# The inverse of chunks 0 to 3 in blocks of 16 instead of one back substitution over 32

## The chip, the cores and the metric

The kernel runs on one core of one Trainium2 chip. The metric is the device time of one launch in microseconds (us), taken as the median of several runs. A profile is one such execution, recorded instruction by instruction; it has a span of its own.

## What is computed

The reference is a recurrent attention block (RWKV-7) with an activation block behind it. Shapes: batch 4, 8 heads, 768 steps, head dimension 40; then 3072 tokens of width 320 through a layer of width 2048.

```python
for t in range(S):                     # per batch and head, state is D x D
    y[t] = r[t] @ state
    Sa = state @ a[t]                  # einsum('bhde,bhe->bhd')
    state = state * w[t][None, :] - outer(Sa, b[t]) + outer(v[t], k[t])
x = y as (3072, 320)
h = x @ w_in
out = (h * cos(h)) @ w_out
```

`w_in` and `w_out` arrive as float64; everything else is float32.

## The kernel before

**Chunks.** The 768 steps are cut into 24 chunks of C = 32 steps. The four batches lie in four blocks of 32 partitions, so one instruction works on 4 batches, and 8 heads lie along the free axis. Within a chunk the recurrence becomes a triangular system: for each batch and head a 32x32 strictly triangular matrix N of products of a and b (decays put in) is needed, and the inverse of the unit triangular matrix made of it. Inverses are made for four chunks at a time, which is 4 x 4 x 8 = 128 systems, one to a partition.

**The steps of a chunk** (names as in the code). `p1_w`, `p1_a`, `p1_b`, `p1_n` prepare two chunks at once: transposed decays `wb`, `aT`, `bT`, and in `p1_n` the products `nps`, which ACT copies into `nt` (L447). `p2_v`, `p2_k`, `p2_g` transpose v, r, k and make the `gram` products, masked by DVE into `ag` and `vvm`. `ch_t` transposes the states `qz`; `ch_q` multiplies them by r; `ch_x` makes the right-hand sides `x0`; `ch_s` multiplies them by the inverse `rt` (products `sps`) and has ACT and DVE take them to `sm`; `ch_z` makes the new states (`dps`; DVE adds at L656 and L663, POOL multiplies by the decay at L657 and L668).

**The inverse.** `inv_start` transposes `nt` into `u` (L460), so that each partition holds one system. `inv_step(j)` for j = 31 down to 1 is one step of back substitution: an outer product of j by (32 - j) elements into `inv_tmp` (L468), and its subtraction from `inv` (L472). `inv_end` transposes `inv` back into `rt` (L476), four chunks in one tile. All of it runs on DVE.

**The weights.** 20 pieces of 128 x 512 float64 numbers are rounded to float32 in the kernel, in four kinds of step: fetch (SP issues the DMA into a tile `words`, L233), taken (DVE L241 and L242, ACT L245 and L247), mantissa (DVE L251, ACT L254), product (DVE L257, POOL L260 for the sign). The `words` tiles share buffers with other tiles: pieces 0 and 1 with `gT`, 2 with `nt`, 3 with `u`, 4 with `inv`, so that pieces 2, 3 and 4 can be fetched only when the first inverse is through with these. The parts of `w_in_sb` and `w_out_sb` that are written last serve as early buffers for w, a and b of chunks 2 and 3.

**The order.** The program is scheduled by hand: each engine runs its instructions in the order in which the Python code issues them, and waits on semaphores where data are missing. `step(work, of_inv, of_w)` does one segment, then counts down the waiting jobs given to `later(n, job)` (mostly loads, to be issued n segments on), then takes `of_inv` steps off the list `inv_steps` and `of_w` off the list `w_steps`. The loop over c at the end lists the segments of each chunk; `M` stands for a place where a piece of the activation block (`first_a`, `first_b`, `second`: products `ph` and `po`) is done. The prologue before it does the preparation of chunks 0 to 3, the inverse, and v, k, g of chunks 0 and 1. SP's queue issues nearly all loads, in order. `busy(n)` issues n matmuls on zeros, and `shifted(n)` n tiny ones on PE.

Lines that matter below: L170 and L175 the scan of decays, L180 its store to `wd` and L152 the loads of w, a, b, k, v, r, L392 `bn`, L490 the POOL copies `vp` and `rp`, L497 and L498 `kn` and v in `vvm`, L541 and L547 the masks of gram, L600 DVE's copy of `x0`, L732 and L740 DVE's part of the cosine.

Of the kernel before, what the change touches and what calls it, by code (L numbers as in the profile page):

```python
# [9 lines left out]
F32 = mybir.dt.float32  # L10
# [10 lines left out]
def kernel(  # L21
# [43 lines left out]
    nc = tc.nc  # L65
# [50 lines left out]

    late = DFF - 2 * H * DP
    late_out = w_out_sb.rearrange("p f n -> p (f n)")[:, NF * DM - 2 * H * DP :]
    nat = {}
    for n, fill in (("w", 1.0), ("a", 0.0), ("b", 0.0)):  # L120
        for i in range(4):
# [310 lines left out]
    def p1_n(c):  # L432
        ps = at("nps")
        for i in range(2):
            for j in range(4):
                for bb in range(B):
                    for e in range(2):
                        mm(
                            ps[blk[bb ^ e], e, (4 * i + j) * C : (4 * i + j + 1) * C],
                            G["bT", c + i][half[e], j, blk[bb]], G["aT", c + i][half[e], j, blk[bb]],  # L440
                            i == 0 and j == 0,
                        )

        if c % 4 == 0:
            G["nt"] = sb1.tile([P, C, 4, 2, HH], F32, tag="nt", name="nt")
        for e in range(2):
            nc.scalar.copy(  # L447
                G["nt"][:, :, c % 4 : c % 4 + 2, e, :].rearrange("p t c j -> p c j t"),
                ps[:, e, : 2 * HH * C].rearrange("p (c j t) -> p c j t", c=2, j=HH),
            )  # L450
        if c % 4 == 2:
            G["inv"] = sb1.tile([P, C * C], F32, tag="inv", name="inv")
            nc.gpsimd.memset(G["inv"], 0.0)
            nc.gpsimd.memset(G["inv"][:, :: C + 1], -1.0)
# [16 lines left out]
        )  # L471
        nc.vector.tensor_tensor(x[:, j:, :j], x[:, j:, :j], tmp, ALU.subtract)  # L472

    def inv_end(c):
        rt = sb2.tile([P, 4, H, C], F32, tag="rt", name="rt")
        nc.vector.transpose(  # L476
            rt.rearrange("p c h t -> p t (c h)"), G["inv"].rearrange("p (t s) -> p t s", t=C)
        )
        for i in range(4):
            G["rt", c + i] = rt[:, i]  # L480

    def inverse(c):
        return [
# [324 lines left out]
    def scanned(q):  # L808

        ws_scan(q)  # L810
        later(2, lambda: ws_store(q))
        if q + 1 < NCH // 4:
            later(12, lambda: ws_fetch(q + 1))
# [17 lines left out]
    with tc.manual_schedule():  # L831
# [46 lines left out]
        first, other = p1(0), p1(2)  # L878
        for seg in (*first[:2], *other[:2], *first[2:], *other[2:]):
            step(seg)  # L880
        scanned(1)
        p2_in(0)
        p2_kn(0)
        inv_steps.extend(inverse(0))
        v, k, g = p2(0)
        v1, k1, g1 = p2(1)
        for n, seg in ((12, v), (0, k), (0, g), (6, main(0)[2]), (6, None), (4, v1), (0, k1), (0, g1)):
            for _ in range(n):
                inv_steps.pop(0)()
            if seg:  # L890
                step(seg)
            else:
                for m in range(3):
                    w_work[m][0]()
                p2_in(1)
                p2_kn(1)
        N_PAD = {0: 111, 19: 75}
        shifted(N_PAD[0])
        while inv_steps:
            inv_steps.pop(0)()  # L900
            if 2 < len(inv_steps) < 9:
                busy(1, True)
        for m in range(3, 5):
            w_work[m][0]()

        done = 0

# [9 lines left out]
            return done < len(pieces) and 2 * pieces[done][0] + 2 <= c  # L917

        M = object()
        for c in range(NCH):  # L920
            t, q, x, s, z = main(c)
            v, k, g = p2(c + 1) if c + 1 < NCH else [lambda: None] * 3
            q0 = c - c % 4 + 4
            fill, pn, pn4 = (1, 4), None, None
            if c == 0:
                segs = [s, z]
            elif c == 1:
                segs = [t, v, q, k, x, g, s, z]
            elif c == 2:
                segs, fill = [t, v, q, k, M, x, M, g, M, s, M, z, M, M], (0, 2)  # L930
            elif c == 3:
                pw4, pa4, pb4, pn4 = p1(4)
                pw, pa, pb, pn = p1(6)
# [39 lines left out]
            for i, seg in enumerate(segs):  # L973
                while seg is s and ("rt", c) not in G:
                    if allowed(c):
                        piece(4, 0)
                    else:
                        inv_steps.pop(0)()
                while seg is pn4 and w_steps:
                    w_steps.pop(0)()  # L980
                if seg is not M:
                    step(seg, *fill, small=seg in (q, x, g, s, z, pn, pn4))
                    if c < 2 or c == 2 and not done:
                        busy({s: 6, q: 5, v: 4, k: 4, z: 4}.get(seg, 3))
                else:
                    place += 1
                    if place * empty // places > (place - 1) * empty // places:
                        continue
                    if allowed(c) and (c != 4 or done < 23):
                        piece(*fill)  # L990
                while i == n - 1 and c > 3 and done < goal and c != 4 and allowed(c):
                    piece(*fill)
                if seg is pn and (c == 3 or c > 4 and c % 4 == 2):
                    inv_steps.extend(inverse(q0))
# [36 lines left out]
```

## Time and profile before

Three runs took 819.85, 822.35 and 826.33 us; the median is 822.35.

| | |
|---|---|
| median of the runs | 822.35 us |
| span of the profiled execution | 823.7 us (mean granted TensorE clock 0.948) |
| PE busy | 746.9 us, 91% of the span |
| PE weight loads | 571.3 us, 69% |
| DVE busy | 509.3 us, 62% |
| ACT busy | 383.8 us, 47% |
| POOL busy | 201.3 us, 24% |
| the inverse's steps on DVE | L472: 72.0 us x186, L468: 70.0 us x186 |
| HBM | 42.07 MB read, 11.14 MB written |

The page also cuts the span into 40 slices of 20.6 us and gives the busy share of each in tenths:

```profile
PE   3656778899689999999999999999999999999997
DVE  6987887859645599354797553895444874332231
PEclk9757799899789999999999999999999999999999
```

The first eight to ten slices are the start: the first chunks, the first inverse and the rounding of the weights. Then PE's row stays at 9.

A row of a table of groups has line, engine, operation, tiles written and read, shapes, count, then busy time. A row of a timeline has start, length, engine, line, operation, tiles, and in brackets the idle time of the engine before it and what ended it. A row of the chain of waits has start, length and who held the chain; SPq and PEq are queues, "issue" is time in which an engine waited for nothing that the profile shows.

### The profile page before, as it was taken

How to read it: one execution, taken by the hardware profiler on the slowest of the kernel's cores; microseconds unless marked ns; L12 is line 12 of the kernel's file. 1: busy time of each engine (PE TensorE's matmuls, PEld its weight loads, DVE VectorE, ACT ScalarE, POOL GpSimd, SP SyncE). 2: the span in 40 equal slices, each digit the busy share in tenths (PEclk: the TensorE clock that was granted, in tenths of full speed). 3: DMA queues.
4: the chain of work that ended last, by engine and by line, in shares of the span. 5: the costliest groups of instructions: out<-in, count | busy, mean ns of one | idle time of the engine just before them, and what ended most of it. 6: DMA issues, size and time to landing. Idle time of an engine off the chain costs nothing.

```text
span 823.7 us, 37673 instructions
## 1 busy us (share of the span) xinstructions
PE 746.9 (91%) x16832; PEld 571.3 (69%) x16832; DVE 509.3 (62%) x1081; ACT 383.8 (47%) x707; POOL 201.3 (24%) x352
## 2 busy tenths in 40 slices
PE   3656778899689999999999999999999999999997
PEld 2534456677467777778777777777787777777775
DVE  6987887859645599354797553895444874332231
ACT  1214676544244553545446446435635445363352
POOL 5315554430214023212221230330330222201000
PEclk9757799899789999999999999999999999999999
DMA  8456663244043322333223323214310212101000
GB/s 120 78 132 168 173 162 104 46 119 69 25 98 84 64 59 52 69 100 65 54 37 71 68 63 67 61 37 65 66 41 24 45 35 52 21 21 37 20 17 16
DMA packets 183297, 55.66 MB, mean 68 GB/s; under 512 B 157152, under 2 KB 178656, under 8 KB 183136
## 3 DMA queue, kind: packets, MB, share of 16 engines
q1 hardware_dynamic: 180560, 51.95, 29.2%
q8 instruction: 132, 2.16, 1.1%
q10 hardware_dynamic: 2320, 0.98, 0.6%
q0 software_dynamic: 256, 0.33, 0.2%
q14 instruction: 29, 0.24, 0.1%
HBM read 42.07 MB, written 11.14 MB: 65 GB/s over the span
## 4 chain that ended last, share of the span: by engine, by line
PE 63%; DVE 19%; ACT 6%; DMA 4%; issue 3%; SPq 3%; POOL 1%; DVEq 0%; ACTq 0%; POOLq 0%
PE ph L101 22%; PE po L101 20%; DVE inv_tmp L468 4%; DVE inv L472 4%; PE x0ps L101 3%; PE dps L101 3%; SPq L152 3%; PE gram L101 2%; DVE rw L391 2%; PE vT L326 2%; PE sps L101 2%; PE qps L101 1%; DVE turns L732 1%; PE nps L101 1%; PE sT L558 1%
## 5 line engine op out<-in xcount | busy, mean ns | idle before, releaser
L101 PE MATMUL po<-w_out_sb,gT 128*128 128x320 f32 x768 | 227.0, 445 | 0.0
L101 PE MATMUL ph<-xT,w_in_sb 128*128 128x256 f32 x768 | 189.5, 393 | 4.8 <-DVE gT L740 3.8
L101 PEld LDWEIGHTS po<-w_out_sb,gT 128*128 128x128 f32 x768 | 142.4, 193 | 55.9 <-issue 4.2
L101 PEld LDWEIGHTS ph<-xT,w_in_sb 128*128 128x128 f32 x768 | 142.3, 194 | 33.9 <-issue 13.9
L730 ACT ACTIVATE turns<-ph,rnd 128x512 f32<-128x512 f32 x96 | 63.8, 685 | 157.2 <-PE ph L101 156.7
L732 DVE SCALAR_TENSOR_TENSOR turns<-turns,ph 128x512 f32<-128x512 f32 x96 | 63.8, 684 | 109.2 <-ACT turns L730 108.9
L740 DVE TENSOR_TENSOR gT<-ph,turns 128x512 f32<-128x512 f32 x96 | 65.6, 685 | 36.3 <-ACT turns L737 36.3
L657 POOL TENSOR_TENSOR qz<-qz,wc 128x160 f32<-128x160 f32 x92 | 43.2, 489 | 163.1 <-DVE qz L656 162.6
L472 DVE TENSOR_TENSOR inv<-inv,inv_tmp 128x31 f32<-128x31 f32 (+15 forms) x186 | 72.0, 387 | 6.4
L468 DVE TENSOR_TENSOR inv_tmp<-u,inv 128x31 f32<-128x31 f32 (+15 forms) x186 | 70.0, 376 | 4.4
L736 ACT ACTIVATE turns<-turns 128x512 f32<-128x512 f32 x96 | 60.2, 627 | 23.3 <-DVE turns L732 23.3
L737 ACT ACTIVATE turns<-turns,half_pi 128x512 f32<-128x512 f32 x96 | 69.3, 722 | 3.1
L490 POOL COPY vp<-nat_v 128x320 f32<-128x320 f32 x25 | 12.5, 501 | 182.9 <-DMA nat_v<-in_v_dram 144.1
L101 PE MATMUL ph<-xT,w_in_tail 64*128 64x256 f32 x384 | 54.8, 404 | 0.0
L656 DVE TENSOR_TENSOR qz<-dps,qz 128x160 f32<-128x160 f32 x92 | 28.9, 315 | 33.9 <-PE dps L101 33.8
L391 DVE RECIPROCAL rw<-nat_w 128x320 f32<-128x320 f32 x20 | 42.8, 2142 | 0.1
L562 ACT COPY s<-sT 128x512 f32<-128x512 f32 x46 | 24.5, 584 | 37.6 <-PE sT L558 37.6
L101 PEld LDWEIGHTS ph<-xT,w_in_tail 64*128 64x128 f32 x384 | 33.3, 187 | 10.4 <-issue 6.6
L668 POOL TENSOR_TENSOR yt<-yt,wb 128x512 f32<-128x512 f32 x24 | 31.3, 1306 | 22.4 <-DVE yt L663 22.4
L546 ACT COPY vvm<-gram 128x256 f32<-128x256 f32 x24 | 8.8, 368 | 55.6 <-DVE ag L541 55.3
L101 PEld LDWEIGHTS sps<-x,rt 32*32 32x32 f32 x1536 | 18.1, 109 | 21.6 <-issue 16.5
L101 PE MATMUL sps<-x,rt 32*32 32x72 f32 x1536 | 23.0, 240 | 10.7 <-DVE rt L476 9.0
(118 smaller groups left out, 1070.1 us busy)
## 6 DMA issues: line engine op xcount, KB each, us to landing
words<-in_moe_w_in_dram SPq DMA_DIRECT2D x8, 512.0 KB
nat_k<-in_k_dram SPq DMA_DIRECT2D x96, 40.0 KB
nat_v<-in_v_dram SPq DMA_DIRECT2D x96, 40.0 KB
nat_r<-in_r_dram SPq DMA_DIRECT2D x96, 40.0 KB
xd<-yt SPq DMA_DIRECT2D x48, 80.0 KB
out_dram<-ot SPq DMA_DIRECT2D x24, 160.0 KB
nat_b<-in_b_dram SPq DMA_DIRECT2D x88, 40.0 KB
wd<-ws SPq DMA_DIRECT2D x5, 640.0 KB
```

The source lines that it names most:

```text
L101: nc.tensor.matmul(o, lhsT=lhsT, rhs=rhs, start=start, stop=stop, skip_group_check=True)
L391: nc.vector.reciprocal(rw, wn)
L468: nc.vector.tensor_tensor(tmp, u[:, j : j + 1, :j].to_broadcast([P, C - j, j]), x[:, j:, j : j + 1].to_broadcast([P, C - j, j]), ALU.mult,)
L472: nc.vector.tensor_tensor(x[:, j:, :j], x[:, j:, :j], tmp, ALU.subtract)
L656: nc.vector.tensor_tensor(z, pick(dp, 0, (2 * N72 + C, 2), (N72, 2), (1, D)), z, ALU.add)
L657: nc.gpsimd.tensor_tensor(z, z, wc.rearrange("p (f m b) -> p f m b", f=2, m=2)[:, :, :, bb] .unsqueeze(3).to_broadcast([P, 2, 2, D]), ALU. ...
L668: nc.gpsimd.tensor_tensor(yt.rearrange("p j b t -> p (j b) t"), yt.rearrange("p j b t -> p (j b) t"), wx, ALU.mult)
L730: nc.scalar.activation(n, u, ACTF.Identity, bias=rnd, scale=1.0)
L732: nc.vector.scalar_tensor_tensor(n, n, -ROUND, u, ALU.add, ALU.subtract)
L736: nc.scalar.activation(n, n, ACTF.Abs)
L737: nc.scalar.activation(n, n, ACTF.Sin, bias=half_pi, scale=-2.0 * math.pi)
L740: nc.vector.tensor_tensor(gT[:, 2 * e : 2 * e + 2].rearrange("p f t -> p (f t)"), us[e], ns[e], ALU.mult)
```

## The change

For chunks 0 to 3 the back substitution runs over two diagonal blocks of 16 at once: `pair_step(j)`, j = 15 to 1, works on 2 x j x (16 - j) elements by one pair of instructions. The block below the diagonal is made by two products on PE per system: `pair_turn` transposes the upper block's inverse into `rn`; `pair_first` multiplies the part of N below the diagonal by it and ACT copies the result to `half`; `pair_second` multiplies the lower block's inverse into that, and DVE adds it to `rt`. Chunk 0's products are made in the prologue, those of chunk 1 in chunk 1's segments, those of chunks 2 and 3 together in chunk 2's. `half` and `rn` lie in columns of `w_out_sb` that the rounding writes late (pieces 13 to 15). The products need N untransposed, so ACT copies `nps` a second time, into `noff`.

Beside that the order of the start changes: the fetches of pieces 0 and 1 are issued before the scan and of piece 2 after chunk 0's x; v and k of chunk 1 move behind the padding of PE, between the pair steps; g of chunk 1 moves behind chunk 0's s, and s and z of chunk 0 move from the loop into the prologue, without fill matmuls. The padding is 121 instead of 111 tiny matmuls, and chunk 2 takes three weight steps per segment instead of two. The inverses of the later chunks are unchanged.

```diff
@@ -116,6 +116,10 @@
 
     late = DFF - 2 * H * DP
     late_out = w_out_sb.rearrange("p f n -> p (f n)")[:, NF * DM - 2 * H * DP :]
+    spare = w_out_sb.rearrange("p f n -> p (f n)")[:, NF * DM - 2 * H * DP - 3 * P * 4 : NF * DM - 2 * H * DP]
+    half0 = spare[:, : 8 * P].rearrange("p (n t) -> p n t", t=C)
+    rn0 = spare[:, 8 * P :].rearrange("p (n t) -> p n t", t=C // 2)
+    nc.gpsimd.memset(half0[:, :, C // 2 :], 0.0)
     nat = {}
     for n, fill in (("w", 1.0), ("a", 0.0), ("b", 0.0)):
         for i in range(4):
@@ -443,11 +447,19 @@
 
         if c % 4 == 0:
             G["nt"] = sb1.tile([P, C, 4, 2, HH], F32, tag="nt", name="nt")
+            if c < 4:
+                G["noff"] = sb2.tile([P, 4, 2, HH, C], F32, tag="rt", name="noff")
         for e in range(2):
             nc.scalar.copy(
                 G["nt"][:, :, c % 4 : c % 4 + 2, e, :].rearrange("p t c j -> p c j t"),
                 ps[:, e, : 2 * HH * C].rearrange("p (c j t) -> p c j t", c=2, j=HH),
             )
+        if c < 4:
+            for e in range(2):
+                nc.scalar.copy(
+                    G["noff"][:, c % 4 : c % 4 + 2, e, :, :].rearrange("p c j t -> p c (j t)"),
+                    ps[:, e, : 2 * HH * C].rearrange("p (c n) -> p c n", c=2),
+                )
         if c % 4 == 2:
             G["inv"] = sb1.tile([P, C * C], F32, tag="inv", name="inv")
             nc.gpsimd.memset(G["inv"], 0.0)
@@ -471,13 +483,75 @@
         )
         nc.vector.tensor_tensor(x[:, j:, :j], x[:, j:, :j], tmp, ALU.subtract)
 
-    def inv_end(c):
+    def inv_end(c, part=False):
         rt = sb2.tile([P, 4, H, C], F32, tag="rt", name="rt")
         nc.vector.transpose(
             rt.rearrange("p c h t -> p t (c h)"), G["inv"].rearrange("p (t s) -> p t s", t=C)
         )
-        for i in range(4):
+        G["rts"] = rt
+        for i in range(0 if part else 4):
             G["rt", c + i] = rt[:, i]
+
+    HB = C // 2
+
+    def pair_step(j):
+        u, x = G["u"], G["inv"]
+        n = HB - j
+        down = HB * C + HB
+        tmp = sb1.tile([P, 16 * 17], F32, tag="inv_tmp", name="inv_tmp")
+        tmp = tmp[:, : 2 * j * n].rearrange("p (h t s) -> p h t s", h=2, s=j)
+        nc.vector.tensor_tensor(
+            tmp, pick(u, j * C, (down, 2), (0, n), (1, j)),
+            pick(x, j * C + j, (down, 2), (C, n), (0, j)), ALU.mult,
+        )
+        to = pick(x, j * C, (down, 2), (C, n), (1, j))
+        nc.vector.tensor_tensor(to, to, tmp, ALU.subtract)
+
+    def pair_turn(c):
+        if c == 0:
+            G["rn"], G["half"] = rn0, half0
+        else:
+            raise NotImplementedError
+        nc.vector.transpose(
+            G["rn"].rearrange("p n u -> p u n"), pick(G["inv"], 0, (1, HB), (C, C)),
+        )
+
+    def pair_first(c, lo, hi):
+        ps = (ps_h if c == 0 else ps_a).tile(
+            [P, 512] if c == 0 else [P, 2, 512], F32, tag="h" if c == 0 else "at", name="aps1")
+        ps = ps if c == 0 else ps[:, 0]
+        nt = G["noff"].rearrange("p c e j t -> p (c e j) t")
+        for n in range(H * lo, H * hi):
+            for g in range(B):
+                mm(ps[blk[g], HB * n : HB * (n + 1)], nt[blk[g], n, :], G["rn"][blk[g], n, :], n == H * lo)
+        nc.scalar.copy(
+            G["half"][:, H * lo : H * hi, :HB],
+            ps[:, H * lo * HB : H * hi * HB].rearrange("p (n u) -> p n u", u=HB),
+        )
+
+    def pair_second(c, lo, hi):
+        ps = (ps_o if c == 0 else ps_a).tile(
+            [P, 512] if c == 0 else [P, 2, 512], F32, tag="o" if c == 0 else "at", name="aps2")
+        ps = ps if c == 0 else ps[:, 0]
+        rt = G["rts"].rearrange("p c h t -> p (c h) t")
+        for n in range(H * lo, H * hi):
+            for g in range(B):
+                mm(ps[blk[g], HB * n : HB * (n + 1)], G["half"][blk[g], n, :], rt[blk[g], n, HB:], n == H * lo)
+        to = rt[:, H * lo : H * hi, HB:]
+        nc.vector.tensor_tensor(
+            to, to, ps[:, H * lo * HB : H * hi * HB].rearrange("p (n u) -> p n u", u=HB), ALU.add
+        )
+        for i in range(lo, hi):
+            G["rt", c + i] = G["rts"][:, i]
+
+    def by_blocks(c):
+        return [
+            inv_start, *(lambda j=j: pair_step(j) for j in range(HB - 1, 0, -1)),
+            lambda: pair_turn(c), lambda: inv_end(c, True),
+        ]
 
     def inverse(c):
         return [
@@ -878,30 +952,43 @@
         first, other = p1(0), p1(2)
         for seg in (*first[:2], *other[:2], *first[2:], *other[2:]):
             step(seg)
+        for m in range(2):
+            w_work[m][0]()
         scanned(1)
         p2_in(0)
         p2_kn(0)
-        inv_steps.extend(inverse(0))
+        inv_steps.extend(by_blocks(0))
         v, k, g = p2(0)
         v1, k1, g1 = p2(1)
-        for n, seg in ((12, v), (0, k), (0, g), (6, main(0)[2]), (6, None), (4, v1), (0, k1), (0, g1)):
+        s0, z0 = main(0)[3:]
+        for n, seg in ((6, v), (0, k), (0, g), (4, main(0)[2])):
             for _ in range(n):
                 inv_steps.pop(0)()
-            if seg:
-                step(seg)
-            else:
-                for m in range(3):
-                    w_work[m][0]()
-                p2_in(1)
-                p2_kn(1)
-        N_PAD = {0: 111, 19: 75}
+            step(seg)
+        w_work[2][0]()
+        p2_in(1)
+        p2_kn(1)
+        N_PAD = {0: 121, 19: 75}
         shifted(N_PAD[0])
         while inv_steps:
             inv_steps.pop(0)()
-            if 2 < len(inv_steps) < 9:
+            if len(inv_steps) == 6:
+                step(v1)
+            elif 2 < len(inv_steps) < 6:
                 busy(1, True)
+            elif len(inv_steps) == 2:
+                step(k1)
+            elif len(inv_steps) == 1:
+                step(lambda: pair_first(0, 0, 1))
         for m in range(3, 5):
             w_work[m][0]()
+        w_steps.pop(0)()
+        step(lambda: pair_second(0, 0, 1))
+        w_steps.pop(0)()
+        w_steps.pop(0)()
+        step(s0)
+        step(g1, 0, 2)
+        step(z0, 0, 3)
 
         done = 0
 
@@ -917,17 +1004,23 @@
             return done < len(pieces) and 2 * pieces[done][0] + 2 <= c
 
         M = object()
+        parts0 = [
+            lambda n=n, f=f: f(0, *n) for n in ((1, 2), (2, 4)) for f in (pair_first, pair_second)
+        ]
         for c in range(NCH):
             t, q, x, s, z = main(c)
             v, k, g = p2(c + 1) if c + 1 < NCH else [lambda: None] * 3
             q0 = c - c % 4 + 4
-            fill, pn, pn4 = (1, 4), None, None
+            fill, pn, pn4, parts = (1, 4), None, None, []
             if c == 0:
-                segs = [s, z]
+                segs = []
             elif c == 1:
-                segs = [t, v, q, k, x, g, s, z]
+                parts = [parts0[0], parts0[1]]
+                segs = [t, parts[0], v, q, parts[1], k, x, g, s, z]
+                fill = (1, 4)
             elif c == 2:
-                segs, fill = [t, v, q, k, M, x, M, g, M, s, M, z, M, M], (0, 2)
+                parts = parts0[2:]
+                segs, fill = [t, parts[0], v, q, k, M, x, M, parts[1], g, M, s, M, z, M, M], (0, 3)
             elif c == 3:
                 pw4, pa4, pb4, pn4 = p1(4)
                 pw, pa, pb, pn = p1(6)
@@ -979,8 +1072,8 @@
                 while seg is pn4 and w_steps:
                     w_steps.pop(0)()
                 if seg is not M:
-                    step(seg, *fill, small=seg in (q, x, g, s, z, pn, pn4))
-                    if c < 2 or c == 2 and not done:
+                    step(seg, *((0, 0) if seg in parts else fill), small=seg in (q, x, g, s, z, pn, pn4))
+                    if seg not in parts and (c < 2 or c == 2 and not done):
                         busy({s: 6, q: 5, v: 4, k: 4, z: 4}.get(seg, 3))
                 else:
                     place += 1
```

## The prediction

> **What bounds the kernel now.** I began with the table of busy time by stretch, to see which engine sets the pace where.
>
> ```profile
> 34.00:63.00 29.00, 13.33 (x450) 9.66 (x448) 25.90 (x71) 4.08 (x9) 3.47 (x6) 0.50 0.56 127
> 63.00:77.00 14.00, 8.38 (x218) 4.75 (x219) 10.08 (x24) 5.57 (x10) 6.16 (x8) 0.74 0.68 179
> 77.00:100.00 23.00, 17.52 (x490) 10.38 (x493) 18.52 (x31) 16.85 (x30) 13.81 (x12) 0.79 0.65 176
> 213.00:823.00 610.00, 595.86 (x13435) 460.26 (x13435) 338.40 (x737) 283.79 (x528) 122.91 (x220) 0.99 0.24 51
> ```
>
> The columns are length, then busy us of PE, PE's weight loads, DVE, ACT and POOL, the granted clock, the DMA share and GB/s. From 213 us on PE is busy 596 of 610 us: the change touches nothing there, so all that it can win lies before, and arrives as a shift. From 34 to 63 us DVE is busy 25.9 of 29 us, and that is the inverse of chunks 0 to 3. It looks like the bound. The chain of waits, in order of time (start, length, what), says otherwise:
>
> ```profile
> 39.09 0.20 DVE inv_tmp L468
> 39.29 3.08 DMA wd<-ws
> ...
> 49.18 0.45 SPq L233
> ...
> 50.15 6.43 DMA words<-in_moe_w_in_dram
> ...
> 58.44 1.86 SPq L152
> ...
> 64.79 1.71 SPq L152
> ...
> 69.03 2.51 DMA nat_r<-in_r_dram
> ```
>
> At 39.3 us, in the middle of the inverse, the chain leaves DVE for good and goes to SP's queue, which issues one 40 KB load each 0.49 us until r of chunk 2 lands at 71.5 us. POOL's timeline shows who waits for that:
>
> ```profile
> 71.69 0.45 POOL L490 COPY rp<-nat_r 128x320 f32<-128x320 f32 x1 [1.24 <-DMA nat_r<-in_r_dram]
> 72.11 1.59 POOL L260 TENSOR_TENSOR w_in_sb<-w_in_sb,sign 128x512 f32<-128x512 f32 x1
> 73.66 2.97 POOL L657 TENSOR_TENSOR qz<-qz,wc 128x160 f32<-128x160 f32 x4
> ```
>
> and PE's that the states `qz` then release the transposes of chunk 1 (5.03 us idle before them). The first words queued behind those loads on SP are the fourth and fifth weight pieces, first issued at 69.58 us. DVE's timeline has the other chain:
>
> ```profile
> 61.18 1.91 DVE L476 STREAM_TRANSPOSE rt<-inv 128x1024 f32<-128x1024 f32 x1
> 76.23 0.68 DVE L241 TENSOR_SCALAR mant<-words 128x512 int32<-128x512 int32 x1
> ```
>
> The second row is DVE's first reading of the fourth piece. So two chains run beside each other and end within a few us: DVE (inverse, then rounding) and SP (loads, then words). Shortening one is worth only the distance to the other.
>
> [...] the trace agrees (31 elements 0.19 us, 256 elements 0.42 to 0.43), so the halves are not free: an instruction of 30 elements still costs 0.19. [...] DVE's L241 on 512 elements takes 0.42 us at 65.47, but 1.37 at 72.61, while POOL was at L260.
>
> **The change, part by part.** Inverse on DVE: 31 pairs of steps go. The page has 72.0 and 70.0 us for 186 instructions each, six inverses, so 23.7 us per inverse. 15 pairs with 2j(16-j) elements come, from 30 up to 128. Old pairs start 0.46 (31 elements), 0.51 (60), 0.57 (87), 0.62 (112) and 0.67 us (135) apart; read off between those, the fifteen sum to 8.7 us. Added on DVE: a transpose of 512 elements, not in the trace; between 0.65 us (half of `u`'s 1.25) and 1.0 (half of `rt`'s 1.91), I take 0.8. An addition from PSUM per group, 128, 128 and 256 elements; nearest rows L663 with 0.28 and L541 with 0.41, so 1.0 us in all, 0.3 of it before chunk 0's s step. **DVE ends chunk 0's inverse 23.7 - 8.7 - 0.8 - 0.3 = 13.9 us earlier**, at 49.2 us instead of 63.1.
>
> PE gets 64 products of 32x32x16 per chunk. Bounds are nps (128 in 1.29 us, 10 ns each) and sps (64 in 1.25 us, 20 ns each): 0.65 to 1.25 us per chunk. Those of chunk 0 are on the short path from `rt` to s and lie beside `rt`'s transpose for one half; the 192 others sit among fill matmuls and PE's idle time in chunks 1 and 2, cost 0, and 2 to 4 us if that cover were gone. ACT copies `noff` four times (L546's 0.37 to L447's 0.55 each): they stand ahead of `bT`, `vT` and `kT` copies and delay u's transpose by some 0.3 us and chunk 0's gram by 1.5, inside the DVE gain that isn't used anyway. ACT's four small copies of `half` are of L546's size or smaller, beside other work. POOL's memset of 512 elements is half of L453's 0.96 us, in time before 15.9 us when POOL waits for DVE.
>
> SP: two whole pieces of words (512 KB each) move from 49.18 us to right behind r of chunk 0, about 27 us, where SP now idles until 31.5 for `kn`. What they pass: kvr of chunk 1, the store of `ws`, w and a. Nothing waits on them there. Chunk 1's loads come behind 1 MB; at 290 to 375 GB/s (the stretches where words flowed, in the DMA view of 40 to 75 us) that is 3 to 3.5 us, over before v of chunk 1 is issued at 34.2. Gained after 49 us: their issues with the gap between, 49.18 to 50.62, **1.44 us**; the wait of a's last load for the second piece[...], 54.78 to 56.60, **1.8**; and possibly the two long issues at 58.44 and 64.79, 1.86 and 1.71 against 0.45, 2.7 together[...]. Similar long issues at 45.25 and 35.62 had no such pieces ahead, so I count none and keep 2.7 for the far end. So the fourth piece is first issued at 69.58 - 3.3 = 66.3 (far end 63.6), the second half 0.5 later, lands 2.5 us on (nat_r's 2.51): 69.8, or 67.1. DVE now reaches that row at 76.23: gain **6.4 to 9.1 us**.
>
> Would DVE be there? From the end of `rt` to 76.23 it takes 13.1 us now, and 1.2 more for chunk 1's gram to come in: 49.2 + 0.6 (a round of products) + 14.3 = 64. So DVE, then stuck in order at that reading, idles some 5 us, and the next late thing is the words. v of chunk 2, on PE at 78.45 us now, is gated by POOL's `rp`, which follows r's landing at 71.5 - 3.3 = 68.2: earlier by 9, so not the later one. s and z of chunk 0 move ahead of POOL's wait for v and r of chunk 2, so the states no longer queue behind it. PE then waits idle at v of chunk 2, and fill matmuls of s and z are gone; its clock may fall, as it has between 34 and 63 us (0.50), at no cost while POOL and DVE set the time.
>
> Chunk 2: three pieces of weight work after each step instead of two; 7 moved forward out of chunk 3. The 20 pieces cost DVE some 60 us (L241, L242, L251 and L257 added up) in 75 such steps, so 5 to 6 us are put before chunk 2's tail and taken off chunk 3's head, which DVE also fills (24.3 of 30 us busy between 120 and 150). I take 0, bounds -2 and +3. The products of chunks 2 and 3 wait for one POOL sign product in the same scratch columns, 1.5 us, behind 4 us of w_in matmuls: 0.
>
> **Sum**: middle of 6.4 to 9.1, 7.8, less 0.7 for the later additions: **7 us**. The profiled execution spans 823.65 us; 816.6 for its like. Its span is 1.3 above the median of the runs (822.35), inside their 819.85 to 826.33, so against the median 815.3.
>
> **Rivals.**
> *The whole DVE gain arrives*: SP catches up too (long issues gone, landings in 2 us)[...]. 24 loads of 0.49 us after the third piece, out at 51.3, end at 63 at best; the fourth piece is there at 65.5, gain 10.7, and 811.5 or a little less. For it: DVE's stretch is the busiest; against: the long issues at 35 and 45 us had no words ahead.
> *Hidden*: SP's load rate is set by the landings, not by the two pieces, or the chunk 2 regrouping gives it back; gain 0 to 3, 819 to 822.
> *Slower, by PE's instruction stream*: PE shows stops that nothing released, 2.51 us at 57.39, 1.24 at 89.62, 1.14 at 93.89, 0.90 at 111.33; the second and third are 128 matmuls apart[...]. After 145 us none longer than 0.3 us shows[...]. If the altered stream laid a stop of 1.1 us in the open at each, up to 120 us; from 7 on the gain is gone, from 14 on it is slower by 1%; with 20, 815 + 22 = 837. Against it: the change adds 256 products and 10 pad matmuls and drops 8 fill matmuls, 258[...], so later stops keep their place.
> That the change doesn't do what it says: the lower block could be late for chunks 1 to 3, and s wait; products are placed two steps or more ahead, so I give it no chance of its own.
>
> **Numbers.** Forecast 0.63, whole gain 0.11, hidden 0.13, slower 0.13. 1% of the median, about what a measurement of this kernel can tell from no change, is 8.2 us: 814.1. Of the forecast's own range (811.5 to 819) 0.38 lies below that, 0.24 in chance; with the first rival 0.35. Slower by over 1% is the last rival, 0.13. Within: 0.52. The range leaves out the last rival and the tail of the first: 810.5 to 822.5.
>
> **What would show it.** DVE has 30 short pair instructions and ends `rt` near 49 us; the chain of waits from 39 to 70 us is still SP's; DVE then idles 4 to 7 us at L241 for DMA words; r of chunk 2 lands near 68. From 213 us on, each row is the same, 7 us earlier. Wrong, if `rt`'s end is on the chain, if the fourth piece lands before DVE wants it, or if PE shows new stops without a releaser.

## The result, and the profile after

| | median of 20 runs | range |
|---|---|---|
| before, on the same chip | 823.0 us | 819.85 to 830.99 |
| changed | 827.56 us | 824.68 to 832.87 |

The ratio is 1.0057, with a 95% interval of 1.0041 to 1.0072: some 4.7 us slower. The prediction said 815.3 us, 810.5 to 822.5. The profiled execution of the changed kernel spans 824.9 us, 1.2 more than the one of before. One pair of profiles is therefore a weak witness of a difference of 4.7; it shows where things moved, and the repeated runs below say what each is worth.

The table of busy time by stretch, of the changed kernel (columns as before):

```profile
34.00:63.00 29.00, 20.96 (x772) 15.69 (x752) 17.23 (x49) 9.48 (x21) 3.12 (x6) 0.56 0.46 96
63.00:77.00 14.00, 11.71 (x323) 8.46 (x324) 11.32 (x20) 5.67 (x11) 9.81 (x12) 0.63 0.73 194
77.00:100.00 23.00, 13.77 (x532) 7.93 (x520) 17.27 (x36) 15.44 (x28) 9.94 (x10) 0.85 0.62 175
213.00:823.00 610.00, 595.89 (x13435) 460.22 (x13435) 338.61 (x737) 283.74 (x528) 122.96 (x220) 0.99 0.24 51
```

The change does what it says: DVE falls from 25.9 to 17.2 us between 34 and 63 us. The last row is that of before to within 0.03 us of PE. So the loss, too, is made before 213 us and arrives as a shift.

The chain of waits of the changed kernel, in order of time:

```profile
41.31 1.50 PE x0ps L101 x63
42.81 1.82 PE pad L101 x70
...
46.90 1.94 PE vT L330 x8
...
54.75 0.30 DVE rt L544
55.09 0.81 PE sps L101 x49
55.91 2.16 issue
58.06 0.46 PE sps L101 x7
58.52 1.42 PE gram L101 x90
59.94 2.13 issue
62.07 0.36 PE gram L101 x7
...
69.39 1.41 DVE mant L245
...
72.77 1.38 DVE mant L245
```

SP's loads, which held this chain from 39 to 72 us before, are gone from it in this execution. It runs over PE and DVE, and 4.3 us of it are two stops of PE that nothing released. DVE's timeline:

```profile
50.93 1.10 DVE L518 STREAM_TRANSPOSE w_out_sb<-inv 128x512 f32<-128x512 f32 x1
51.93 1.90 DVE L488 STREAM_TRANSPOSE rt<-inv 128x1024 f32<-128x1024 f32 x1
54.75 0.29 DVE L544 TENSOR_TENSOR rt<-rt,aps 128x128 f32<-128x128 f32 x1 [0.34 <-PE aps L101]
...
72.77 1.38 DVE L245 TENSOR_SCALAR mant<-words 128x512 int32<-128x512 int32 x1
...
117.87 0.43 DVE L245 TENSOR_SCALAR mant<-words 128x512 int32<-128x512 int32 x1 [3.82 <-DMA words<-in_moe_w_out_dram]
```

`rt` is transposed at 53.8 us instead of 63.1, and chunk 0's part is whole with the addition in the third row, at 55.0. The fourth row is the first reading of piece 3 (the fourth piece; they are counted from 0): 72.77 against 76.23. The last row is new: DVE stands 3.82 us for the words of piece 14. And PE, in the same stretch of its timeline:

```profile
117.06 1.99 PE L101 MATMUL ph<-xT,w_in_sb 128*128 128x256 f32 x8
124.20 1.90 PE L101 MATMUL aps<-rt,w_out_sb 32*32 32x16 f32 x128 [5.14 <-POOL w_out_sb L264]
...
127.98 0.30 PE L101 MATMUL gram<-aT,kT 40*32 40x32 f32 x6 [1.16 <-issue]
```

PE stands 5.14 us before the products of chunks 2 and 3, until POOL has put the sign to a weight piece that shares columns with `half`. Against before, the start of `sps` (the s step) has moved by -8.1 us in chunk 0, -5.5 in chunk 1, +4.4 in chunk 2, +2.7 in chunk 3 and +0.6 in chunk 4. The gain is there early and is lost by x of chunk 2 (`x0ps`), before PE's wait of 5.14 us; first before, then changed:

```profile
114.48 0.88 PE L101 MATMUL x0ps<-vvm,ag 32*32 32x72 f32 x64
114.37 0.88 PE L101 MATMUL x0ps<-vvm,ag 32*32 32x72 f32 x64
```

From there to `sps` of chunk 2 it takes 17.8 us instead of 13.2. Single profiles need care here. `before_fill_three` below has the instructions of the kernel before in the same order until chunk 2; its profile still differs from that of before by 2.1 us where piece 3 is first issued (67.5 against 69.6), by 4.0 at v of chunk 2 and by 2.5 at s of chunk 1.

### The profile page after: what moved, and what is told of

It reads as the page before. It is cut to its first block, busy times and chain, and to the rows that moved or that the text cites. A ratio compares the mean times of both kernels' runs of the same rounds, so it can differ in the third digit from the quotient of the medians.

```text
span 824.9 us, 38687 instructions
## 1 busy us (share of the span) xinstructions
PE 750.2 (91%) x17346; PEld 575.0 (70%) x17346; DVE 497.9 (60%) x1054; ACT 385.3 (47%) x714; POOL 200.2 (24%) x353
## 4 chain that ended last, share of the span: by engine, by line
PE 63%; DVE 19%; ACT 6%; issue 4%; DMA 4%; SPq 2%; POOL 1%; DVEq 0%; ACTq 0%; POOLq 0%
PE ph L101 21%; PE po L101 19%; DVE inv_tmp L480 4%; DVE inv L484 3%; PE x0ps L101 3%; PE dps L101 3%; PE gram L101 3%; PE vT L330 2%; DVE rw L395 2%; PE sps L101 2%; PE nps L101 2%; PE qps L101 1%; DVE turns L806 1%; SPq L156 1%; PE sT L632 1%
## 5 line engine op out<-in xcount | busy, mean ns | idle before, releaser
L101 PE MATMUL ph<-xT,w_in_sb 128*128 128x256 f32 x768 | 186.3, 387 | 3.2 <-issue 1.9
L101 PEld LDWEIGHTS ph<-xT,w_in_sb 128*128 128x128 f32 x768 | 140.4, 191 | 32.0 <-issue 12.5
L811 ACT ACTIVATE turns<-turns,half_pi 128x512 f32<-128x512 f32 x96 | 69.3, 722 | 3.1
L484 DVE TENSOR_TENSOR inv<-inv,inv_tmp 128x31 f32<-128x31 f32 (+15 forms) x155 | 61.0, 393 | 5.3
L480 DVE TENSOR_TENSOR inv_tmp<-u,inv 128x31 f32<-128x31 f32 (+15 forms) x155 | 58.9, 380 | 3.2
L632 PE MATMUL sT<-ident,qz 128*128 128x128 f32 x184 | 27.5, 292 | 6.6 <-DVE yt L737 3.2
```

What stands on the lines that cost most here:

```text
L101: nc.tensor.matmul(o, lhsT=lhsT, rhs=rhs, start=start, stop=stop, skip_group_check=True)
L480: nc.vector.tensor_tensor(tmp, u[:, j : j + 1, :j].to_broadcast([P, C - j, j]), x[:, j:, j : j + 1].to_broadcast([P, C - j, j]), ALU.mult,)
L632: nc.tensor.transpose(ps[:, i // 4, (i % 4) * P : (i % 4 + 1) * P], qz[:, i // 2, i % 2, C : C + P], ident)
L811: nc.scalar.activation(n, n, ACTF.Sin, bias=half_pi, scale=-2.0 * math.pi)
```

## The experiments

All ratios are times divided by that of the kernel before on the same chip (below 1 is faster), from 14 to 22 runs of each kernel (6 and 7 of the three whose interval is half a per cent wide). "Rounding's end" is the start of the last weight piece's product, in the one profile of each kernel (149.1 us before, 146.7 changed).

### What loses time: chunk 2

`fill_two`: the changed kernel with two weight steps per segment in chunk 2. `second_early`: three steps, but the second products of chunks 2 and 3 moved ahead of the rounding that writes their columns. `before_fill_three`: the kernel before, with three steps.

```diff
- segs, fill = [t, parts[0], v, q, k, M, x, M, parts[1], g, ...], (0, 3)
+ segs, fill = [t, parts[0], v, q, k, M, x, M, parts[1], g, ...], (0, 2)   # fill_two
+ segs, fill = [t, parts[0], v, q, parts[1], k, M, x, M, g, ...], (0, 3)   # second_early
```

> The changed kernel with two weight steps per segment in chunk 2, as in the kernel before, instead of three. The second product for chunks 2 and 3 then stands ahead of piece 14 without being moved, and seven weight steps go back to chunk 3. Theory A (wait for the shared columns): as in the run with the product moved, 2.5 to 5 us faster than the changed kernel. Theory B (paced by words and rounding): within 1.5 us of the changed kernel. Theory C (three steps per segment cost chunk 2 more than chunk 3 gives back): 2 us or more faster than the run with the product moved.

> The changed kernel with one segment moved: in chunk 2 the second product for chunks 2 and 3 stands before k instead of after x, so it is issued before piece 14 of the rounding writes the scratch columns that it reads. All else is the same, and so is the number of instructions. Theory A (the gain is lost at that product, where PE stood 5.1 us for POOL's sign product of piece 14): the wait is gone, chunk 2's s step comes 4 to 6 us earlier than in the changed kernel, and half of that or more is left at the end: 2.5 to 5 us faster than the changed kernel, so level with the kernel before or up to 1 us faster. Theory B (chunks 2 and 3 are paced by the words landing and by DVE's rounding, and the product only stood where PE would have waited anyway): the wait goes to another PE row in chunk 2, and the time is within 1.5 us of the changed kernel, 4 us above before.

> The kernel before with only one thing of the change: three weight steps per segment in chunk 2. Theory C (this part alone costs): 2 to 4 us slower than before. Theories A and B: within 1.5 us of before, since what chunk 2 gets more chunk 3 gets less.

| | ratio | 95% |
|---|---|---|
| `fill_two` | 0.9991 | 0.9974 to 1.0008 |
| `second_early` | 1.0067 | 1.0045 to 1.0088 |
| `before_fill_three` | 0.9996 | 0.9979 to 1.0014 |

The third step per segment makes all the difference between the changed kernel and the one before: 1.0057 / 0.9991 = 1.0066. In the kernel before, where it was expected to cost 2 to 4 us if it costs by itself, it costs nothing. The wait for the shared columns, plain as it looks in the trace, is not what costs the time. In `second_early` it is gone, and PE's timeline shows a longer wait further on, at a place where the kernel before waits 3.76 us. First the kernel before, then `second_early`:

```profile
124.14 3.65 PE L101 MATMUL ph<-xT,w_in_sb 128*128 128x256 f32 x8 [3.76 <-DVE gT L740]
```

```profile
123.28 0.73 PE L101 MATMUL gram<-rT,vT 40*32 40x32 f32 x62
134.08 3.66 PE L101 MATMUL ph<-xT,w_in_sb 128*128 128x256 f32 x8 [10.07 <-DVE gT L814]
```

DVE sits in the rounding between, and `gT` queues behind it. As the profiles have it, three steps put more work on DVE ahead of the last segments of chunk 2: from rounding's end to `sps` of chunk 3 it is 6.3 to 7.1 us with two steps and 11.1 to 12.9 with three, so rounding must end about 5 us earlier to pay for it. In `before_fill_three` it does (143.3, 5.8 earlier). In the changed kernel it ends 3.0 earlier than in `fill_two` (146.7 against 149.7). This is an account read off one profile each; the runs show only which edit costs the time.

### Is the shorter inverse worth anything by itself?

`before_half_inverse` is the kernel before with steps j = 31 to 16 of the first inverse left out (so the inverses of chunks 0 to 3 are not whole), which spares DVE 13 us and moves nothing else. `before_half_inverse_pool` also moves the 16 loads of a and b of chunks 4 and 5 from SP's queue to POOL's. `before_pool_loads` moves the loads only.

```diff
+        inv_steps[1:17] = [lambda: None] * 16
-    load(c + 2 + m % 2, "wab"[m // 2])
+    load(c + 2 + m % 2, "wab"[m // 2], nc.gpsimd if c == 2 and m > 1 else nc.sync)
```

> The kernel before, with steps 31 to 16 of the first inverse left out (they are the first sixteen on DVE; the inverse of chunks 0 to 3 is then not the reference's, the rest is untouched). DVE is spared 13 us and nothing is put in its place: no products on PE, no new order, no copies. Theory SP (what is issued in order on SP's queue sets the pace from 40 us on): rt ends some 11 us earlier, DVE then waits for the words of piece 3, and the time falls by 1 to 3 us. Theory DVE (the inverse is on the path and the change gave its gain away elsewhere): the time falls by 8 us or more.

> As the run with half of the first inverse left out, and 16 loads of SP's queue (a of chunk 4, a and b of chunk 5, b of chunk 4) issued from POOL's queue, which is idle between 44 and 69 us. SP issues piece 3 some 8 us earlier. Theory SP: now the shorter inverse pays: 4 us or more faster than the run without the moved loads, 6 to 9 us faster than before. If something else than SP holds chunk 1: within 1.5 us of the run without the moved loads.

> The kernel before, whole inverse, with only the 16 loads (a of chunk 4, a and b of chunk 5, b of chunk 4) issued from POOL's queue. Theory SP and DVE side by side, 3 us apart: r of chunk 2 lands some 7 us earlier, but DVE, with its inverse ending at 63 us, reaches the fourth piece at 75 or later; so only some 1 to 3 us of the 5 us that the same loads gave with half of the inverse left out. Rival (SP alone sets the pace, the inverse is hidden twice over): the whole 4 to 6 us, so that no shorter inverse is needed.

| loads of a and b on | whole inverse | half of it |
|---|---|---|
| SP | 1 | 0.9996 (0.9981 to 1.0011) |
| POOL | 1.0013 (0.9998 to 1.0028) | 0.9937 (0.9916 to 0.9958) |

Either alone is worth nothing that these runs can tell from noise (1 to 3 us had been expected of each), both together 0.6%. That is what two chains side by side look like. The first DVE row is `before_half_inverse`, at the words of piece 3:

```profile
74.27 0.61 DVE L241 TENSOR_SCALAR mant<-words 128x512 int32<-128x512 int32 x1 [7.60 <-DMA words<-in_moe_w_out_dram]
```

and the same row with the loads moved:

```profile
68.19 0.43 DVE L241 TENSOR_SCALAR mant<-words 128x512 int32<-128x512 int32 x1 [1.37 <-DMA words<-in_moe_w_out_dram]
```

SP issues these words at 70.29 us in the first and at 63.17 in the second. Without the loads moved, DVE's spare 13 us end in a wait of 7.6 us, and v of chunk 2 starts at 78.5 us as in the kernel before.

### Does the early fetch help alone?

`before_fetch_early`: the kernel before, pieces 0 and 1 fetched ahead of the scan.

```diff
             step(seg)
+        for m in range(2):
+            w_work[m][0]()
         scanned(1)
...
-                for m in range(3):
-                    w_work[m][0]()
+                w_work[2][0]()
```

> The kernel before with only one thing of the change: the fetches of weight pieces 0 and 1 are issued right behind r of chunk 0, that of piece 2 stays. The prediction had SP gain 3.3 us on what is issued after 49 us, and r of chunk 2 land so much earlier. If SP's loads set the pace until 70 us as predicted, the states of chunk 1 come 2 to 3 us earlier (DVE's own chain is 3 us behind SP's) and the time falls by 1 to 3 us. If DVE's inverse and rounding set the pace, nothing moves: within 1 us.

It gave 0.9998 (0.9984 to 1.0013). SP first issued piece 3 at 65.8 us, 3.8 earlier than before, but DVE, with the whole inverse before it, read it at 78.0 (76.2 before). So SP was relieved in this profile, and alone that is worth nothing, as the table above would have it.

### Relieving SP in the changed kernel

`fill_two_pool_loads` is `fill_two` with the 16 loads on POOL's queue; `after_pool_loads` the same with three steps. `fill_two_ws_late` leaves the loads on SP and puts the fetch of the next decays `ws`, which SP issues at 72 to 74 us and so ahead of piece 7, six segments later; `fill_two_pool_ws` does both.

```diff
-            later(12, lambda: ws_fetch(q + 1))
+            later(18 if q == 1 else 12, lambda: ws_fetch(q + 1))
```

> The changed kernel with two weight steps per segment in chunk 2, and the same 16 loads issued from POOL's queue. Against the run with two steps alone, DVE's wait of 5 us for piece 3 goes. Theory SP: 3 to 6 us faster than before. Rival (PE's stops without a releaser and the words of pieces 7 to 14 take it back by chunk 2): within 1.5 us of before, as with two steps alone.

> The changed kernel as it is, three weight steps per segment in chunk 2, with the 16 loads issued from POOL's queue. If three steps cost because DVE, in order, stands at pieces 13 to 15 for their words while chunk 2's own rows queue behind, the cost stays: SP's early relief doesn't bring those later words sooner by itself, so 3 to 5 us slower than two steps with the moved loads (0.6% faster than before): level with before, within 2 us. If three steps cost only where SP is late from the start: 4 to 6 us faster than before, like two steps.

> The changed kernel with two weight steps per segment in chunk 2, and the next fetch of the decays (640 KB) six segments later, so that chunk 0's result, which SP writes out and then waits for before it can issue piece 7, doesn't land behind it. If that wait (5 us on SP, 75 to 80 us) is where the early gain goes: piece 7 is issued 3 us or more earlier, DVE doesn't wait for it, and the time is 1 to 3 us below before. If not: within 1 us of the run with two steps alone.

> The changed kernel with two weight steps per segment in chunk 2, the 16 loads on POOL's queue, and the next fetch of the decays six segments later: both relieve SP at different places (before 70 us; 75 to 80 us). If they add up: 6 to 8 us faster than before (0.6% and 0.3%). If the second only mends what the first has made early already: within 1 us of the moved loads alone, 5 us faster than before.

| | ratio | 95% | piece 3 first issued, read by DVE |
|---|---|---|---|
| `fill_two` | 0.9991 | 0.9974 to 1.0008 | 70.4, 74.1 |
| `fill_two_pool_loads` | 0.9941 | 0.9913 to 0.9969 | 58.9, 69.4 |
| `fill_two_ws_late` | 0.9971 | 0.9957 to 0.9984 | 67.0, 72.4 |
| `fill_two_pool_ws` | 0.9963 | 0.9943 to 0.9983 | 59.2, 71.3 |
| `after_pool_loads` | 1.0008 | 0.9990 to 1.0026 | 58.9, 68.5 |

`fill_two_pool_loads` is the best version of this study, 819.1 us against 824.2 for the kernel before beside it. It has 7 runs, and its profile is that of the fastest of them. The same short inverse pays once SP is relieved and the third step is gone. What the later fetch is worth stays open: 0.9971 is not clear of 0.9991, and in its profile piece 7 is issued 5.0 us earlier than in `fill_two` (79.1 against 84.1), but SP was 3.4 us ahead at piece 3 already, before the edit acts. The two reliefs don't add up. And the third step costs the same here: 1.0008 / 0.9941 = 1.0067.

### Why the third step costs in the changed kernel and not in the one before

DVE's wait for piece 14 is the suspect: on SP those words stand behind the loads of k of chunk 4. `after_kvr4_pool` moves k, v and r of chunk 4 to POOL's queue. `after_kvr4_late`, `after_pool_kvr4_late` and `fill_two_pool_kvr4_late` issue them six segments later, which turned out too late for r: POOL copies `nat_r` at 134.24 us in `after_kvr4_late` and SP issues its loads at 134.91, so chunk 4 is computed with chunk 3's r in these three, and what they time is not the same computation. `after_kvr4_four`, `after_pool_kvr4_four` and `fill_two_kvr4_four` issue them four segments later, ahead of the copies.

```diff
-  later(3 + i if c > 1 else 1, lambda n=n: load(c + 1, n))
+  later((7 if c == 3 else 3) + i if c > 1 else 1, lambda n=n: load(c + 1, n))
```

> The changed kernel as it is, three weight steps per segment in chunk 2, with k, v, r of chunk 4 (12 loads between the words of pieces 13 to 16 on SP, 111 to 120 us) issued from POOL's queue. If three steps cost because DVE stands for those words (3.8 us at piece 14) with chunk 2's rows behind: piece 14 comes 2 us earlier, and the time is 2 to 4 us below the changed kernel. If the cost is the reordering as such, not the words: within 1 us of the changed kernel.

> The changed kernel as it is, three weight steps per segment in chunk 2, with k, v, r of chunk 4 issued six segments later on SP's own queue, so that the words of pieces 14 to 16 go ahead of them and no other queue is loaded (in the run that put them on POOL's queue, POOL's sign products came late). If three steps cost because DVE stands for words in chunk 2: the wait at piece 14 falls from 3.8 to 2 us or less, rounding ends 1.5 us or more earlier, and the time is 1.5 to 4 us below the changed kernel. If the order of rows on DVE costs by itself: rounding may end earlier, but the time stays within 1 us of the changed kernel.

> The changed kernel with two weight steps per segment in chunk 2, the 16 early loads on POOL's queue, and k, v, r of chunk 4 six segments later. With two steps DVE doesn't stand for words in chunk 2 once the early loads are moved, so the later loads should change little: 4 to 6 us below before, within 1 us of the moved early loads alone. If words still paced it: 6 us or more below before.

> The changed kernel with three weight steps, and only the loads of k, v and r of chunk 4 issued four segments later, still ahead of the copies that read them; the computation is whole. Theory (the third step costs because the words of piece 14 are late, behind the k loads of chunk 4 on SP's queue): DVE's 3.8 us wait for piece 14 shrinks below 1 us, rounding ends some 3 us earlier than 146.7, the ratio falls from 1.0057 to 1.000 to 1.003. Rival (the third step costs by the order of work on PE and DVE alone, words or no words): the wait shrinks but the ratio stays at 1.005 to 1.007.

> The control: the changed kernel with two weight steps in chunk 2 (0.9991) and the same later loads; the computation is whole. Theory: with two steps the words of piece 14 were not late, so nothing moves: 0.997 to 1.001. If later loads of chunk 4 are a gain or a loss of their own, it shows here: rival 0.993 to 0.996, or 1.002 to 1.005; and the distance to the run with three steps is then the third step's cost without the word wait.

> The changed kernel with three weight steps, the 16 loads of a and b on POOL's queue (1.0008 so) and k, v and r of chunk 4 four segments later; the computation is whole. Theory: DVE's wait for piece 14 (3.78 us with the loads moved) goes, rounding ends some 3 us earlier than 140.4, ratio 0.994 to 0.998. Rival (order of work alone): the wait goes, 1.000 to 1.002.

| loads of chunk 4 | three steps | two steps |
|---|---|---|
| in place | 1.0057 (1.0041 to 1.0072) | 0.9991 (0.9974 to 1.0008) |
| four later | 1.0026 (1.0010 to 1.0042) | 1.0001 (0.9985 to 1.0017) |
| in place, a and b on POOL | 1.0008 (0.9990 to 1.0026) | 0.9941 (0.9913 to 0.9969) |
| four later, a and b on POOL | 0.9988 (0.9969 to 1.0007) | |
| six later, a and b on POOL | 0.9985 (0.9969 to 1.0001) | 0.9984 (0.9968 to 1.0000) |

`after_kvr4_late`, six later with a and b on SP, gave 1.0028 (1.0013 to 1.0043). `after_kvr4_pool` gave 1.0065 (1.0041 to 1.0090): the wait for piece 14 fell to 1.62 us, but PE's wait for POOL's sign product rose to 7.00, with loads on POOL's queue as well; it decides nothing.

The clean pair is the second row. DVE's row in `after_kvr4_four`:

```profile
117.51 0.43 DVE L245 TENSOR_SCALAR mant<-words 128x512 int32<-128x512 int32 x1 [2.09 <-DMA words<-in_moe_w_out_dram]
```

The wait shrank from 3.82 to 2.09 us, not below 1 as expected, and rounding's end did not move (146.8). But the ratio fell by 0.3%, and the distance between three steps and two from 0.66% to 0.25%, while with two steps the later loads gain nothing. So the order of these loads on SP takes part in the third step's cost, though the profile doesn't show by which wait. With a and b on POOL the four segments give 0.9988 against 1.0008, within the noise and between the two expectations. How much of the rest is DVE's queue at the end of chunk 2, and how much is words still late, stays open, and so does why later loads cost the best version 0.4% (0.9941 to 0.9984; that profile has a PE stop of 4.5 us in chunk 3's gram, and the kernel reads r too early).

## Why the prediction was wrong, step by step

**Two chains side by side: right.** The two-by-two table shows it. It is also why the inverse gains nothing alone.

**DVE 13.9 us earlier: partly.** The 30 pair instructions are busy 9.0 us (predicted 8.7), the additions 0.29, 0.28 and 0.42 us (predicted 1.0 in all), the transpose 1.10 (0.8). But in this profile `u` is transposed at 36.23 us, 2.8 later than before (the copies of `noff` on ACT, taken as 0.3, and a PE stop of 2.55 in `nps`), and the pairs take 13.3 us from first to last: other work lies between, and 1.49 us of nothing that the trace names. `rt` ended 9.3 us earlier, and with the addition, which the 13.9 include, 8.1. Other profiles are kinder: `rt` ends at 50.5 to 55.3 us in the fourteen of the changed order, 53.1 on average, and at 62.9 to 65.9 in the four with the whole old inverse.

**SP first issues piece 3 at 66.3, 3.3 us earlier: wrong, and the gain failed here first.** It was 68.0, and 70.2 and 70.4 in `second_early` and `fill_two`. The eight profiles of the changed order with a and b on SP have 67.0 to 70.4, 68.8 on average; three of the order before (`before`, `before_fill_three`, `before_half_inverse`) have 67.5 to 70.3, 69.1 on average. So SP gained some 0.3 us in place of 3.3. SP's timeline, the kernel before:

```profile
49.18 3.94 SPq L233 DMA_DIRECT2D words<-in_moe_w_in_dram  x6
53.22 3.69 SPq L152 DMA_DIRECT2D nat_a<-in_a_dram  x4
56.96 5.32 SPq L152 DMA_DIRECT2D nat_b<-in_b_dram  x8
...
64.35 3.14 SPq L152 DMA_DIRECT2D nat_v<-in_v_dram  x4
...
69.58 3.24 SPq L233 DMA_DIRECT2D words<-in_moe_w_out_dram  x7
```

and the changed one:

```profile
50.48 2.48 SPq L237 DMA_DIRECT2D words<-in_moe_w_in_dram  x4
53.05 2.03 SPq L156 DMA_DIRECT2D nat_a<-in_a_dram  x4
55.13 5.71 SPq L156 DMA_DIRECT2D nat_b<-in_b_dram  x8
...
62.92 3.02 SPq L156 DMA_DIRECT2D nat_v<-in_v_dram  x4
...
68.02 4.25 SPq L237 DMA_DIRECT2D words<-in_moe_w_out_dram  x7
```

Both terms of the sum came in: the words give 3.94 - 2.48 = 1.46 us (predicted 1.44), a's loads 3.69 - 2.03 = 1.66 (1.8). What was left out is the start of the stretch: it came 1.30 us later (1.4 on average over the same eight and three profiles), after w was first issued at 43.52 us instead of 42.43 (44.8 and 45.0 in `second_early` and `fill_two`). I had written that nothing waits on what the words were moved past. Whether the moved words made it late is not shown: `before_fetch_early` has the same early words, and there w goes out at 41.65 and the stretch begins at 48.92. And the long issues stayed, as I had assumed. That relief of SP was missing is shown by `fill_two_pool_loads` against `fill_two`: with piece 3 issued at 58.9 us instead of 70.4, the same short inverse gives 0.9941 instead of 0.9991.

**DVE waits 4 to 7 us for these words: in part.** DVE's timeline in `fill_two`:

```profile
74.15 0.62 DVE L245 TENSOR_SCALAR mant<-words 128x512 int32<-128x512 int32 x1 [5.02 <-DMA words<-in_moe_w_out_dram]
```

In `second_early` it is 5.69, in the four variants that move loads of chunk 4 but not a and b it is 1.1 to 3.1. In the profiles of the changed kernel and of `fill_two_ws_late` no wait is left to see; in the first, DVE itself stood 2.87 and 2.36 us for PE, which its two stops had made late. In these eight profiles piece 3 is read 2.1 to 4.0 us earlier than before, not 6.4 to 9.1. That was the term of the sum that was mis-sized.

**v of chunk 2 is not the later one: right.** It starts at 71.9 us, 6.5 earlier. But by x of chunk 2 the gain is gone (114.37 us against 114.48; 115.5 in `fill_two`), and what took the rest of it is not shown. Late words are one suspect: piece 7 is issued at 82.2 us (78.9 before), since z of chunk 0, moved ahead, now puts the loads of `xT` before it on SP; their store goes out at 73.65 us, but they only at 80.53 (before: 78.07 and 80.91), and piece 7 behind them. PE's stops are the other: between `sps` of chunk 1 and x of chunk 2 the changed kernel has 2.49 and 1.73 us of them, the kernel before 1.14 and 0.90.

**Three weight steps in chunk 2 cost 0, between -2 and +3: wrong.** The distance between `fill_two` and the changed kernel is 0.66%, 5.4 us. It turned "no change" into "slower". I had counted steps moved from chunk 3 to chunk 2 and found DVE equally full in both, but did not ask whether the words could be there in time, nor what stands behind DVE at the end of chunk 2. From x to `sps` of chunk 2 it takes 17.8 us in the changed kernel and 12.6 in `fill_two`.

**The wait for the shared columns costs 0: right in the outcome, wrong in the reason.** It is 5.14 us in the trace, not hidden; but taking it away gains nothing.

**The sums.** 66.3 + 0.5 + 2.5 is 69.3, not 69.8, so the forecast gain should have read 6.9 to 9.6 us, which is no nearer to the result. The two products of a chunk are 128 PE instructions together, not 64: PE has 17,346 matmuls instead of 16,832, 514 more where 258 were counted, four blocks of 128 and two. Two of the later stops keep their place: those of 1.24 and 1.14 us, at matmuls 1,230 and 1,358 of the kernel before (counted from 0), are 256 further on in the changed kernel, at 1,486 and 1,614 with 0.97 and 2.49 us, in rows of the same tiles. In chunk 0 the two products take 0.80 and 0.72 us. And the span of a profile is not a launch: the profiled run of the changed kernel spans 824.9 us and took 826.88, so the "1.3 above the median" compared two different things.

**The rivals.** "Hidden" said 819 to 822 us, by SP's rate or by chunk 2's regrouping. SP gained next to nothing, though not for the reason given there, and the regrouping took more than it said; together they went past its end. PE's stops did not come every 128 matmuls: after 150 us they sum to 0.6 us. But in the first 150 us they are 9 with 14.1 us instead of 5 with 6.2 in the two profiles, and this rival stands in part: no run takes the stops away, so how much of the early gain went to them stays open.

## What to carry to other kernels

Where two chains end within a few us of each other, price both before pricing an edit, and test it as a two-by-two: here neither a shorter inverse nor relieved loads moved the time, and both together gave 0.6%. Two profiles of the same instructions can differ by some us at one place, so a shift of that size needs more than one pair of them. A regrouping of filler work is an edit of its own: ask of each piece that moves forward whether its data can be there, and who queues behind it. A long wait in the trace is a suspect only; the one of 5.14 us on PE was worth nothing, because a later wait grew from 3.8 us to 10.

## What was not expected of the hardware

Moving issues to another queue was not free here: SP issues a 40 KB load each 0.49 us (four of k in 1.98 us from 62.37 in the kernel before), POOL each 0.58 (12 of the 16 in 6.9 us in `before_half_inverse_pool`), and the move paid only together with the shorter inverse.

Several of PE's stops without a releaser lie 128 matmuls apart: at 848, 976 and 1,104 in the changed kernel, and at 1,486 and 1,614. Their lengths vary from kernel to kernel: the one before the last six matmuls of chunk 3's gram took 1.16 us in the changed kernel and 1.47 to 2.05 in five of its variants. Over one profile each, all such stops sum to 8.1 us on average in the six kernels with the order of before (5.3 to 11.0), and to 13.9 in the fourteen with the changed order (9.0 to 18.5); in all twenty, 0 to 3.8 us of it lie after 150 us. They don't decide the ratios alone: `fill_two_ws_late` has 17.3 us of them at 0.9971, `second_early` 9.1 at 1.0067. The profiles list an instruction queue, q8, with 132 packets in the kernel before and 136 in the changed one, which have 33,664 and 34,692 matmuls and weight loads on PE. If those packets are PE's, which the profiles don't say, dividing gives an estimate of 255 instructions to a packet, or some 128 matmuls with their loads, near the distance of those stops. That the packets cause the stops was not tried, nor what part of the stops reaches the end.
